# A planner in place of a hand-written order: causal attention and a feed-forward layer on one core

## The chip, the core and the metric

The kernel runs on one core of a Trainium2 chip. The core has five engines with a queue of their own each: TensorE (PE in the rows; PEld is its weight loads), VectorE (DVE), ScalarE (ACT), GpSimd (POOL) and SyncE (SP), which here issues every DMA. Each engine takes its instructions strictly in the order in which they stand in its queue. The metric is the device time of one execution, in microseconds.

## The reference

Four batches of 448 positions, 12 heads of 64. Causal attention in fp32, then layer normalising, then a feed-forward layer of width 3072 with a residual:

```python
scores = scale * np.matmul(q, k.transpose(0, 1, 3, 2))
scores = np.where(mask, -1000000000.0, scores)
scores = scores - np.max(scores, axis=-1, keepdims=True)
attn = np.exp(scores)
attn = attn / (np.sum(attn, axis=-1, keepdims=True) + 1e-09)
attn_out = np.matmul(attn, v)
x = attn_out.transpose(0, 2, 1, 3).reshape(B, S, H * D)
xn = (x - mu) / np.sqrt(var + 1e-06) * g_ln
return x + np.maximum(xn @ w_ch1, 0.0) @ w_ch2
```

The weights w_ch1 and w_ch2 arrive as 64-bit floats; the kernel makes fp32 of them on the chip.

## The kernel before

**Split products.** A large product is done in three passes: each operand is split into a high part (rounded to the fast matmul format, `wh`, `xh`, `hh`, `kh`) and a low part (the rest: `wl`, `xl`, `hl`, `kl`), and high x high, high x low and low x high are added in one PSUM bank. Making a pair of parts is a cast on ACT (L152, L659) and a subtraction on DVE (L156, L660) or POOL (L254, L425, L714).

**Attention** (class `Att`) goes by pairs of heads, six in a batch. For a pair: scores `sc` (L278 in full fp32 for batch 0, L285 split for the others), mask and row minimum on DVE (L293), exponential with its sum on ACT (L307), reciprocal on DVE and normalising (`norm`, L323, on POOL for batch 0, else on DVE), transposes `pt` of P on TensorE (L339), whose result is copied from PSUM to `PT` by ACT (L342) or DVE (L344), as a table `ev` says, and the product with V, `px` (L358): four blocks of columns (448, 336, 224, 112) for each of the two heads, which write to different halves of the bank. `stats` transposes x (`pln`, L371) for mean and variance.

**The stages.** Batch 0's attention stands alone at the start. Then `ffn` runs batches 0 and 1 (`ph` L490 to the hidden layer, `po` L509 out of it: 2 x 864 matmuls of 448 columns). In its `yield`s, once for 18 matmuls, pieces of the attention of batches 1, 2 and 3 are issued. In between, each weight tile is converted (L125, L129, L136), split, and stored: `scratch` holds the fp32 weight, `kept` both split parts, for later use. Last comes class `Pair`: batches 2 and 3 together by a scheme with 7 products in place of 8 on blocks. A group of it has two blocks of the first kind (7 products of 9 matmuls) and three of the second (7 of 6), 2 x 63 + 3 x 42 = 252 matmuls, and there are six groups. Sums of weight blocks (`s`, on POOL, L642) are split afresh (`wp`), single blocks are read from `kept` (`wk`). The products land in banks `bX`, `bY`, `bA`; `after1` combines them (copies `p1`, `u2`, `p5`, `b11`, `b22`, `b21` to SBUF on ACT, L706; sums on DVE, L709, L714, L717) and splits the hidden layer into `h1`, `h2`, `hx` parts; `after2` adds to `xT` (L779).

**What sets the order.** All by hand: tables at the top give each step of a head pair its slot (`SAT`, `TAT`, `NAT`, `END`, `STARTS`), a slot is one step of the loop over weights, and what is called first in a slot stands first in every queue it uses. `weights_ahead` places conversion and split some slots early; `Pair` loads and splits a set number of products ahead and lets a few steps lag by one or two products (`then`).

Of the kernel before, what the change touches and what calls it, by code (L numbers as in the profile page):

```python
# [1 line left out]

# [32 lines left out]
GAP = 6  # L35
FIRST = -20
# [21 lines left out]

@with_exitstack
def kernel(ctx, tc, qk, v, w1, w2, g, out):  # L60
    nc = tc.nc

    def pool(name, bufs, **kw):
        return ctx.enter_context(tc.tile_pool(name=name, bufs=bufs, **kw))
# [4 lines left out]
    ps_open, conv_open, att_open = ExitStack(), ExitStack(), ExitStack()  # L69
    ps = ps_open.enter_context(tc.tile_pool(name="ps", bufs=2, space=PSUM))  # L70
    conv = conv_open.enter_context(tc.tile_pool(name="conv", bufs=1))
    ap = att_open.enter_context(tc.tile_pool(name="ap", bufs=1, side="right"))
    late = []
# [16 lines left out]
    kept = [dr.tile([P, 2, UH], F32, name=f"kept{i}") for i in range(ns)]  # L90
# [54 lines left out]
    def keep_parts(s):  # L145
        for part, w in ((0, wh), (1, wl)):
            nc.sync.dma_start(out=kept[s % ns][:, part, :], in_=w[s].bitcast(F32))

    def split1(s):
        assert s in ready or s >= ns  # L150
        wh[s] = sb.tile([P, UH], F32R, tag="wh", name="wh", bufs=4)
        nc.scalar.activation(out=wh[s], in_=w32[s], func=ACTF.Copy)  # L152
# [7 lines left out]
    def open_late(_):  # L160
        conv_open.close()
        late.append(pool("late", 1, reuse_waits="tile"))

    def weights_ahead(start):
# [9 lines left out]
        for s in range(2 * ns):  # L174
            if s >= ns + KEEP0:
                put(s - 3, (load_parts, s))
                continue
            t = (-EARLY + GAP * s, *ELAG) if s < early else (s - 4, 1, 2, 3)
            put(t[0] + t[3], (split2, s))
            if s >= KEEP0:  # L180
# [24 lines left out]
    class Att:  # L205
# [31 lines left out]
        def split1(self, p):  # L237
# [5 lines left out]
            nc.scalar.activation(out=qs, in_=rq, func=ACTF.Copy)  # L243
            nc.vector.tensor_copy(kh, rk)  # L244
# [68 lines left out]
        def norm(self, p, h):  # L313
# [7 lines left out]
            for i in (0, 1, 3, 2):  # L321
                pp = self.t["P", p, h][:, OFF[i]:OFF[i + 1]]
                eng.tensor_scalar(  # L323
                    out=pp, in0=pp, scalar1=r[:, i:i + 1], scalar2=1.0,
                    op0=ALU.mult, op1=ALU.mult,
                )

        def transposes(self, p, grp, eng):
# [12 lines left out]
            if eng == "act":  # L341
                nc.scalar.copy(out=t[:, :o], in_=pt[:, :o])  # L342
            else:
                nc.vector.tensor_copy(t[:, :o], pt[:, :o])  # L344

        def pv(self, p):
# [15 lines left out]
            nc.scalar.copy(out=self.xT[p], in_=px)  # L362
# [49 lines left out]
        def apply1(self, c):  # L412
# [9 lines left out]
            nc.scalar.activation(out=self.xh[:, c, :], in_=t, func=ACTF.Copy)  # L422
# [55 lines left out]
    def ffn(a, s, hh, hl):  # L478
        for f0, f1 in ((0, HF), (HF, NF)):
            for x in range(0, HF, 2):  # L480
# [4 lines left out]
                for k, (y, c) in enumerate(seq):  # L485
                    if k == KC:
                        yield
# [6 lines left out]
                    if c == KC - 1:  # L494
# [4 lines left out]
                        )  # L499
                s += 2  # L500
                yield
            for m in range(KC):
                pm = ps.tile([P, S], F32, tag="mm", name="po", bufs=3)
                for x in range(HF):
                    if x == KC:
                        yield
# [12 lines left out]
    class Pair:  # L519
# [18 lines left out]
        def open_inputs(self):  # L538
            att_open.close()
            self.xp = pool("pair_x", 1, side="right", reuse_waits="tile")  # L540
# [13 lines left out]
        def parts(self, src, hi, lo, eng):  # L554
            nc.scalar.activation(out=hi, in_=src, func=ACTF.Copy)
# [29 lines left out]
        def plan(self):  # L585
# [21 lines left out]
            self.u, self.w, self.bank, self.hid = {}, {}, {}, {}  # L607
# [24 lines left out]
        def combine(self, b):  # L632
            w = self.width(b)
            u = self.u.pop(b)
            u = {(i, k): u[:, i, k * w:(k + 1) * w] for i in range(2) for k in range(2)}
# [9 lines left out]
        def weight_parts(self, n):  # L645
# [5 lines left out]
            t = sb.tile([P, 2, w], F32, tag=("wh", "wl")[n % 2], name="wk", bufs=4)  # L651
            nc.sync.dma_start(out=t, in_=kept[s][:, :, o:o + w])
            self.w[b, k] = t.bitcast(F32R)

        def weight(self, n):
# [3 lines left out]
            nc.scalar.activation(out=t[:, 0, :], in_=src, func=ACTF.Copy)  # L659
# [40 lines left out]
        def after1(self, b, blk, k):  # L700
# [4 lines left out]
            def copy(dst, src, func=ACTF.Copy):  # L705
                nc.scalar.activation(out=dst, in_=src, func=func)  # L706
# [21 lines left out]
            def then(lag, f, *args):  # L728
                self.later.setdefault(self.n + lag, []).append((f, args))
# [71 lines left out]
    with tc.manual_schedule():  # L801
# [4 lines left out]

        def add_batch(b):
# [12 lines left out]
            for mine, whole in ((first, pre), (second, post)):  # L820
                for t, fs in mine.items():
                    whole.setdefault(slot(t), []).extend(fs)
# [9 lines left out]
        make_identity(nc, ident)  # L832
# [9 lines left out]
        for s in range(start, 2 * ns):  # L842
            for b in range(1, B):
# [10 lines left out]
            for f, x in later:  # L854
                f(x)
            if s >= 0:
# [5 lines left out]
                next(feed)  # L862
            for f, args in post.get(s, []):
                f(*args)
# [14 lines left out]
        ps_open.close()  # L879
        psb = pool("psb", 8, space=PSUM, reuse_waits="tile")  # L880
        pair.hidden()
        pair.run()

# [32 lines left out]
```

## Time and profile before

| | us |
|---|---|
| median of 3 runs | 920.6 (918.53 to 920.83) |
| profiled execution | 918.47 |
| its span, first to last instruction | 916.6 |
| TensorE busy in it | 869.5 (95%) |
| DVE busy | 649.8 (71%) |
| ACT busy | 476.7 (52%) |
| POOL busy | 275.7 (30%) |

Busy is the time in which at least one instruction of the engine is at work. Matmuls overlap, each row being longer than the distance to the next, so that a TensorE at 100% is not yet at its best pace. What remains of the 916.6 us is time in which TensorE waits.

### The profile page before, as it was taken

What the parts mean: (1) busy time and instruction counts of PE and PEld (TensorE: products, weight loads), DVE (VectorE), ACT (ScalarE), POOL (GpSimd) and SP (SyncE); (2) the same over time, 40 slices, a digit from 0 to 9 for tenths busy, and PEclk for the clock granted to TensorE, in tenths of its full rate; (3) what the DMA queues carried; (4) which work ended last, traced back from release to release, by engine and by line L of the source; (5) the groups of instructions that cost most, each with busy time, mean ns of one, the idle gap of its engine ahead of it and who ended that gap; (6) DMA issues with size and microseconds to landing.
All of it is one profiled execution on the core that took longest, in us unless ns stands there. A gap on an engine that the chain in (4) does not pass through costs nothing.

```text
span 916.6 us, 13600 instructions
## 1 busy us (share of the span) xinstructions
PE 869.5 (95%) x4662; PEld 749.8 (82%) x4662; DVE 649.8 (71%) x1412; ACT 476.7 (52%) x1050; POOL 275.7 (30%) x274
## 2 busy tenths in 40 slices
PE   6989999999889989989999999899999999999998
PEld 4657988888768768878888889788889898888987
DVE  4876888767778987767667537877575856757585
ACT  6945888779667555544545312352433525243350
POOL 5643111111021221111111004755353525535440
PEclk9999999999899999999999999999999999999999
DMA  9911777768678978776887558635445363644534
GB/s 246 358 57 49 251 284 274 277 245 320 247 247 284 351 256 337 273 256 235 292 290 281 182 182 273 208 113 180 127 139 162 119 193 104 191 128 138 155 91 174
DMA packets 77876, 196.31 MB, mean 214 GB/s; under 512 B 7536, under 2 KB 35184, under 8 KB 77808
## 3 DMA queue, kind: packets, MB, share of 16 engines
q1 hardware_dynamic: 77808, 195.46, 62.1%
q8 instruction: 36, 0.59, 0.3%
q14 instruction: 32, 0.26, 0.1%
HBM read 133.30 MB, written 62.13 MB: 213 GB/s over the span
## 4 chain that ended last, share of the span: by engine, by line
PE 63%; ACT 14%; DVE 14%; DMA 4%; issue 4%; SPq 1%; POOL 0%; ACTq 0%; DVEq 0%
PE ph L490 15%; PE bX L695 14%; PE po L509 13%; PE bY L695 6%; PE px L358 4%; PE bA L695 3%; PE sc L285 3%; PE pt L339 3%; ACT P L307 2%; DVE wp L660 2%; ACT h L706 2%; DMA scratch<-w 2%; DVE w L136 1%; ACT w L125 1%; ACT b L706 1%
## 5 line engine op out<-in xcount | busy, mean ns | idle before, releaser
L254 POOL TENSOR_TENSOR kl<-qkraw,kh 128x896 fp32r<-128x896 f32 x18 | 49.3, 2740 | 294.6 <-DVE kh L244 224.6
L307 ACT ACTIVATE P<-P,nm 112x448 f32<-112x448 f32 (+3 forms) x176 | 91.7, 524 | 47.3 <-DVE nm L293 47.3
L490 PE MATMUL ph<-xh,wh 128*128 128x448 f32 x288 | 107.6, 374 | 0.0
L490 PE MATMUL ph<-xl,wh 128*128 128x448 f32 x288 | 106.4, 369 | 0.7 <-POOL xl L425 0.7
L509 PE MATMUL po<-hh,wh 128*128 128x448 f32 x288 | 106.9, 371 | 0.0
L509 PE MATMUL po<-hh,wl 128*128 128x448 f32 x288 | 105.8, 367 | 0.2 <-DVE wl L156 0.2
L490 PE MATMUL ph<-xh,wl 128*128 128x448 f32 x288 | 105.9, 368 | 0.0
L509 PE MATMUL po<-hl,wh 128*128 128x448 f32 x288 | 105.5, 366 | 0.0
L660 DVE TENSOR_TENSOR wp<-s,wp 128x256 fp32r<-128x256 f32 (+1 forms) x120 | 76.8, 645 | 33.8 <-ACT wp L659 32.2
L659 ACT ACTIVATE wp<-s 128x256 fp32r<-128x256 f32 (+1 forms) x120 | 53.7, 459 | 86.4 <-PE bY L695 41.9
L293 DVE CUSTOM_DVE_ANT_0 P<-sc,mask 112x448 f32<-112x448 f32 (+3 forms) x176 | 70.6, 444 | 29.9 <-PE sc L285 16.6
L714 POOL TENSOR_TENSOR h<-b,h 128x448 fp32r<-128x448 f32 x36 | 41.3, 1148 | 126.8 <-ACT b L706 82.2
L496 DVE SCALAR_TENSOR_TENSOR hl<-ph,hh 128x448 fp32r<-128x448 f32 x48 | 29.8, 623 | 65.8 <-ACT hh L495 65.5
L779 DVE TENSOR_TENSOR xT<-xT,bX 128x448 f32<-128x448 f32 x72 | 44.6, 619 | 34.5 <-PE bX L695 33.9
L339 PE MATMUL pt<-ident,P 112*112 112x112 f32 x440 | 55.0, 261 | 14.1 <-DVE stat L374 8.1
L339 PEld LDWEIGHTS pt<-ident,P 112*112 112x112 f32 x440 | 46.1, 133 | 24.7 <-DVE stat L374 9.3
L642 POOL TENSOR_TENSOR s<-u 128x256 f32<-128x256 f32 (+1 forms) x60 | 57.0, 951 | 25.0 <-DMA u<-scratch 14.7
L490 PEld LDWEIGHTS ph<-xl,wh 128*128 128x128 f32 x288 | 54.7, 190 | 5.6 <-POOL xl L425 1.3
L509 PEld LDWEIGHTS po<-hh,wl 128*128 128x128 f32 x288 | 54.1, 188 | 5.8 <-DVE wl L156 1.1
L490 PEld LDWEIGHTS ph<-xh,wh 128*128 128x128 f32 x288 | 54.7, 190 | 4.9
L509 PEld LDWEIGHTS po<-hh,wh 128*128 128x128 f32 x288 | 54.1, 188 | 5.3
L490 PEld LDWEIGHTS ph<-xh,wl 128*128 128x128 f32 x288 | 54.5, 189 | 4.6 <-DVE wl L156 0.3
(160 smaller groups left out, 2113.5 us busy)
## 6 DMA issues: line engine op xcount, KB each, us to landing
raw<-w_dram SPq DMA_DIRECT2D x39, 768.0 KB, 8.8
scratch<-w SPq DMA_DIRECT2D x48, 384.0 KB, 6.2
kept<-wh SPq DMA_DIRECT2D x48, 384.0 KB, 8.5
kept<-wl SPq DMA_DIRECT2D x48, 384.0 KB, 8.3
qkraw<-qk_dram SPq DMA_DIRECT2D x18, 896.0 KB, 6.1
full<-scratch SPq DMA_DIRECT2D x18, 768.0 KB, 8.7
wk<-kept SPq DMA_DIRECT2D x36, 384.0 KB, 3.8
wk<-kept SPq DMA_DIRECT2D x54, 256.0 KB, 3.2
```

The lines of the kernel that those rows point to most:

```text
L254: nc.gpsimd.tensor_tensor(out=kl, in0=rk, in1=kh.bitcast(F32), op=ALU.subtract)
L293: nc.vector.tensor_tensor_reduce(out=self.t["P", p, h][:, OFF[i]:OFF[i + 1]], in0=pt[:, o:o + n], in1=mask[:, S - n:], op0=ALU.add, op1=AL ...
L307: nc.scalar.activation(out=pp, in_=pp, func=ACTF.Exp, scale=-1.0, bias=nm[:, x:x + 1], accum_out=self.t["sm", p, h][:, i:i + 1],)
L339: nc.tensor.transpose(pt[:, o:o + C], pp[:, a:a + C], ident[:C, :C])
L490: nc.tensor.matmul(pm[y], lhsT=w[:, c * P:c * P + P], rhs=z[:, c, :], start=(c == 0 and i == 0), stop=(c == KC - 1 and i == 2),)
L509: nc.tensor.matmul(pm, lhsT=w[:, o:o + P], rhs=z[:, x, :], start=(x == 0 and i == 0), stop=(x == HF - 1 and i == 2),)
L642: nc.gpsimd.tensor_tensor(out=v[dst], in0=x, in1=y, op=op)
L659: nc.scalar.activation(out=t[:, 0, :], in_=src, func=ACTF.Copy)
L660: nc.vector.tensor_tensor(out=t[:, 1, :], in0=src, in1=t[:, 0, :].bitcast(F32), op=ALU.subtract)
L695: nc.tensor.matmul(pm, lhsT=w, rhs=z, start=(new and c == 0 and i == 0), stop=(c == nk - 1 and i == 2), skip_group_check=True,)
L714: eng.tensor_tensor(out=dst, in0=src, in1=y, op=ALU.subtract)
L779: nc.vector.tensor_tensor(out=t, in0=t, in1=src, op=ALU.add)
```

## The change

The kernel's code now runs twice over, in a sense. First every call of an engine is only written down: `Plan.record` keeps it as a `Task` with the tasks that it depends on (`access` compares the pieces of buffers that are read and written, a PSUM bank as a whole), a price (`cost`) and, for matmuls, a due time: the sum of the matmul prices written down before it. Then `schedule` walks backwards, giving each task the time by which it is needed, and forwards as a list schedule: the engine that is free first takes, of the tasks that are ready, the one needed soonest. Last, `issue` makes the real calls in the order of planned start. In the profile all instructions thus have one line, L398.

Copies between any of SBUF and PSUM (`move`), and the normalising of batches 1 to 3, are written down with two ways (`either`): ACT or DVE, whichever engine takes it; the second way counts as needed 8000 ns later. Each buffer of a pool becomes a place of its own. `ffn` yields after 3 matmuls in place of 9 or 18, so that the attention's steps are written down in finer turn. The lags in `Pair` go. Of split weights only the low part is stored in `kept` and read again; the high part is cast again, from `scratch` (`full`) or from the loaded block `u`, which stays in its buffer for that.

```diff
+    def cost(self, t):
+        n, sbuf = t.size, [x for x in t.ins if x.buf.pool.space is None and x.idx.size > 8]
...
+        if t.engine == "tensor":
+            if t.method == "transpose":
+                return 0.84 * n, 200, False
+            if t.kw["rhs"].dtype == F32R:
+                return max(0.4531 * n + 2.5, 60), 200, False
+            return (0.42 if t.outs[0].p[1] - t.outs[0].p[0] == D else 1.69) * n, 200, False
+        if t.engine == "scalar":
+            return n / 1.4 + 220 + 190 * ("accum_out" in t.kw), 60, False
...
+    def schedule(self):
...
+        for t in (tasks[n] for n in reversed(line)):
+            x = t.due if t.engine == "tensor" else 1e9
+            for m in t.then:
+                x = min(x, need[m])
+            if t.engine == "sync":
+                x -= DMA_SLACK + t.lag / 300
+            elif t.engine and t.engine != "tensor":
+                x -= t.cost + t.lag + SLACK
+            elif t.engine and x < t.due:
+                x -= t.cost + t.lag + SLACK
+            need[t.n] = x
...
+            while soon[e] and soon[e][0][0] <= at:
+                _, n, more = heapq.heappop(soon[e])
+                if n not in start:
+                    heapq.heappush(avail[e], (need[n] + more, n))
+            n = heapq.heappop(avail[e])[1]
...
+            if t.port:
+                at = max(at, port)
+                port = at + t.cost
...
+    def move(dst, src):
+        nc.either(
+            ("scalar", "activation", (), dict(out=dst, in_=src, func=ACTF.Copy)),
+            ("vector", "tensor_copy", (dst, src), {}),
+        )
...
     def load_parts(s):
-        for part, w, tag in ((0, wh, "wh"), (1, wl, "wl")):
-            t = sb.tile([P, UH], F32, tag=tag, name=tag, bufs=4)
-            nc.sync.dma_start(out=t, in_=kept[s % ns][:, part, :])
-            w[s] = t.bitcast(F32R)
+        t = sb.tile([P, UH], F32, tag="wl", name="wl", bufs=4)
+        nc.sync.dma_start(out=t, in_=kept[s % ns])
+        wl[s] = t.bitcast(F32R)
...
-            t = sb.tile([P, 2, w], F32, tag=("wh", "wl")[n % 2], name="wk", bufs=4)
-            nc.sync.dma_start(out=t, in_=kept[s][:, :, o:o + w])
-            self.w[b, k] = t.bitcast(F32R)
+            self.w[b, k] = t = sb.tile([P, 2, w], F32R, tag=("wh", "wl")[n % 2], name="wk", bufs=4)
+            move(t[:, 0, :], self.full[b][LEFT[k]])
+            nc.sync.dma_start(out=t[:, 1, :].bitcast(F32), in_=kept[s][:, o:o + w])
```

**First place: TensorE while batch 0's second half of the hidden layer is made.** `pt` and `pln` go to PSUM banks that ACT or DVE must empty, `sc` are scores of a later pair, `ph` matmuls of the hidden layer. Before:

```order
L339 MATMUL pt<-ident,P 112x112 x8
L371 MATMUL pln<-ident,xT 112x128 x2
L285 MATMUL sc<-kh,qs 112x224
L285 MATMUL sc<-kl,qs 112x224
L285 MATMUL sc<-kh,qs 112x224
L285 MATMUL sc<-kl,qs 112x224
L285 MATMUL sc<-kh,qs 112x448
L285 MATMUL sc<-kl,qs 112x448
L490 MATMUL ph<-xh,wh 128x448
L490 MATMUL ph<-xl,wh 128x448
```

The same transposes and statistics after the change:

```order
L398 MATMUL pt<-ident,P 112x112 x4
L398 MATMUL ph<-xh,wh 128x448
L398 MATMUL ph<-xl,wh 128x448
L398 MATMUL ph<-xh,wl 128x448
L398 MATMUL pt<-ident,P 112x112 x4
L398 MATMUL ph<-xh,wh 128x448
L398 MATMUL ph<-xl,wh 128x448
L398 MATMUL ph<-xh,wl 128x448
L398 MATMUL pln<-ident,xT 112x128 x2
L398 MATMUL ph<-xh,wh 128x448
L398 MATMUL ph<-xl,wh 128x448
L398 MATMUL ph<-xh,wl 128x448
```

The eight transposes, two statistics and six scores stood in one block; now three `ph` stand between each two pieces.

**Second place: ACT at the same transposes.** The two copies `PT<-pt` belong to the eight transposes above. Before:

```order
L125 ACTIVATE w32_2666<-raw_2487 128x768
L129 ACTIVATE bits_2665<-raw_2487 128x768
L152 ACTIVATE wh_2672<-w32_2556 128x768
L495 ACTIVATE hh_1013<-ph_2612 128x448
L342 COPY PT_2695<-pt_2694 112x448
L342 COPY PT_2702<-pt_2701 112x448
```

And after:

```order
L398 ACTIVATE hh_994<-ph_2520 128x448
L398 ACTIVATE P_2409<-P_2409,r_2536 112x224
L398 ACTIVATE P_2581,sm_2600<-P_2581,nm_2582 112x448
L398 ACTIVATE P_2581,sm_2600<-P_2581,nm_2592 112x336
L398 ACTIVATE PT_2617<-pt_2602 112x448
L398 ACTIVATE PT_2623<-pt_2612 112x448
L398 ACTIVATE wh_2631<-w32_2512 128x768
```

The copies stood behind the weight conversion, a cast and the `hh` of the block; now that cast stands behind them.

**Third place: the second block of a group in the pair.** ACT before, where `p1` is the copy of bank bX that lets TensorE go on in that bank:

```order
L706 ACTIVATE h1_6234<-bX_7681 128x448
L706 ACTIVATE h2_6235<-bY_7738 128x448
L706 ACTIVATE p1_7828<-bX_7816 128x448
L706 ACTIVATE h1_6234<-bZ_7771 128x448
L706 ACTIVATE h2_6235<-bA_7833 128x448
```

DVE after, where that copy now stands:

```order
L398 TENSOR_TENSOR bZ_7795<-b21_7830,bZ_7795 128x448
L398 COPY p1_7852<-bX_7828 128x448
L398 TENSOR_TENSOR h2_6351<-bY_7757,h2_6351 128x448
L398 TENSOR_TENSOR wp_7855<-s_7751,wp_7855 128x256
L398 TENSOR_TENSOR h1_6241<-bZ_7795,h1_6241 128x448
L398 TENSOR_TENSOR bA_7850<-bA_7850,p1_7852 128x448
```

The copy has changed engine. Some products later in the same block, DVE before, up to the step `bA<-bY`, from which the hidden layer's parts are made:

```order
L717 TENSOR_TENSOR bY_7870<-bY_7870,u2_7868 128x448
L660 TENSOR_TENSOR wp_7895<-s_7748,wp_7895 128x256
L717 TENSOR_TENSOR bZ_7898<-bX_7816,p5_7883 128x448
L660 TENSOR_TENSOR wp_7916<-s_7748,wp_7916 128x256
L709 SCALAR_TENSOR_TENSOR bA_7833<-bY_7870,b11_7846 128x448
```

And DVE after:

```order
L398 CAST wp_7914<-s_7751 128x256
L398 TENSOR_TENSOR bY_7887<-bY_7887,u2_7890 128x448
L398 TENSOR_TENSOR bZ_7925<-bX_7828,p5_7904 128x448
L398 TENSOR_TENSOR wp_7914<-s_7751,wp_7914 128x256
L398 SCALAR_TENSOR_TENSOR bA_7850<-bY_7887,b11_7885 128x448
```

The subtraction of a weight stands ahead of `bA<-bY` in both; its cast, which ACT did, is now DVE's own.

## Rows read from the trace of the kernel before

**Rows 1.** The windows; columns as the first line says (PEclk: granted clock).

```profile
core 0: us, PE busy (x) PEld busy (x) DVE busy (x) ACT busy (x) POOL busy (x), PEclk, DMA share, GB/s
0.00:79.97 79.97, 66.50 (x383) 44.21 (x383) 52.80 (x181) 52.26 (x148) 38.33 (x72) 0.98 0.61 190
79.97:200.00 120.03, 119.90 (x673) 105.30 (x674) 92.77 (x202) 97.58 (x185) 17.13 (x10) 1.00 0.66 243
200.00:360.00 160.00, 143.96 (x823) 123.84 (x822) 129.54 (x291) 106.25 (x220) 28.60 (x14) 0.98 0.80 292
360.00:585.60 225.60, 221.89 (x1272) 195.04 (x1272) 148.81 (x359) 96.95 (x222) 41.05 (x26) 1.00 0.72 253
585.60:916.60 331.00, 317.25 (x1515) 281.36 (x1513) 225.92 (x382) 123.69 (x277) 150.62 (x154) 1.00 0.47 145
sum 916.60, PE 869.50 PEld 749.76 DVE 649.82 ACT 476.73 POOL 275.74; mean PE 173.90 PEld 149.95 DVE 129.96 ACT 95.35 POOL 55.15
```

**Rows 2.** The chain that ended last: start us, length us, what, count.

```profile
353.23 2.04 PE px L358 x16
381.95 3.67 PE ph L490 x18
...
754.63 1.84 PE bX L695 x9
```

**Rows 3.** TensorE's waits, 200 to 360: us in total, times, longest.

```profile
PE pt L339 <- DVE stat L374: 5.5, 3, 2.4
PE pln L371 <- ACT PT L342: 4.1, 2, 3.7
```

**Rows 4.** TensorE in order of time: start, length, what, [idle before <-releaser].

```profile
235.89 0.93 PE L339 MATMUL pt<-ident,P 112*112 112x112 f32 x8
240.56 0.68 PE L371 MATMUL pln<-ident,xT 128*112 128x128 f32 x2 [3.75 <-ACT PT L342]
...
243.28 0.57 PE L490 MATMUL ph<-xh,wl 128*128 128x448 f32 x1
```

**Rows 5.** ACT in order of time, at the same place.

```profile
237.27 0.89 ACT L125 ACTIVATE w<-raw 128x768 f32<-128x768 f32 x1
...
239.99 0.94 ACT L342 COPY PT<-pt 112x448 f32<-112x448 f32 x2
```

**Rows 6.** DVE in order of time, at the same place.

```profile
240.12 0.62 DVE L496 SCALAR_TENSOR_TENSOR hl<-ph,hh 128x448 fp32r<-128x448 f32 x1 [2.12 <-ACT hh L495]
```

**Rows 7.** The chain, one group of the pair before the row at 754.63.

```profile
700.63 1.84 PE bX L695 x9
```

**Rows 8.** TensorE's first matmuls in order of time, and its last in the chain.

```profile
5.46 8.10 PE L278 MATMUL sc<-first_qk 128*112 128x448 f32 x22 [5.46 <-DMA first_qk<-qk_dram]
...
911.75 1.25 PE bX L695 x6
```

**Rows 9.** TensorE in order of time, in the second block of a group.

```profile
767.89 0.47 PE L695 MATMUL bX<-xT2h,wp 128*128 128x448 f32 x1 [0.41 <-ACT p L706]
```

**Rows 10.** ACT in order of time, at the same place.

```profile
767.26 0.58 ACT L706 ACTIVATE p<-bX 128x448 f32<-128x448 f32 x1
```

**Rows 11.** DVE in order of time, in the block before.

```profile
762.27 1.20 DVE L660 TENSOR_TENSOR wp<-s,wp 128x384 fp32r<-128x384 f32 x1 [1.46 <-ACT wp L659]
763.39 0.62 DVE L709 SCALAR_TENSOR_TENSOR bA<-bY,b 128x448 f32<-128x448 f32 x1
```

**Rows 12.** DVE in order of time, in batch 0's attention.

```profile
45.81 4.05 DVE L251 TENSOR_TENSOR qs<-qkraw,qs 64x896 fp32r<-64x896 f32 x1
```

**Rows 13.** POOL in order of time, at the same place.

```profile
46.84 2.07 POOL L254 TENSOR_TENSOR kl<-qkraw,kh 128x896 fp32r<-128x896 f32 x1
```

**Rows 14.** Groups by line: count | busy us, mean ns | idle before, releasers.

```profile
L660 DVE TENSOR_TENSOR wp<-s,wp 128x256 fp32r<-128x256 f32 (+1 forms) x120 | 76.8, 645 | 33.8 <-ACT wp L659 32.2 <-POOL s L642 1.5
L642 POOL TENSOR_TENSOR s<-u 128x256 f32<-128x256 f32 (+1 forms) x60 | 57.0, 951 | 25.0 <-DMA u<-scratch 14.7 <-DVE xT L779 5.3 <-DVE wp L660 4.6
L659 ACT ACTIVATE wp<-s 128x256 fp32r<-128x256 f32 (+1 forms) x120 | 53.7, 459 | 86.4 <-PE bY L695 41.9 <-PE bX L695 40.4 <-POOL s L642 4.1
```

More of the change, by code (lines that the diff above doesn't have):

```diff
@@ L68, with turn, f @@
     dr = pool("dr", 1, space=DRAM)
[L69 to L73, printed above, removed]
+    ps = pool("ps", 2, space=PSUM)
+    conv = pool("conv", 1)
+    ap = pool("ap", 1, side="right")
+    late = [pool("late", 1, reuse_waits="tile")]
+    pair_x = pool("pair_x", 1, side="right", reuse_waits="tile")
+    psb = pool("psb", 8, space=PSUM, reuse_waits="tile")
+    def turn(old, new):
+        def f():
+            stacks[old.name].close()
+            open_pool(new)
+        plan.change(f, [old], [new])
     ident = const.tile([P, P], F32, name="ident")
@@ L89 @@
     scratch = [dr.tile([P, UE], F32, name=f"scratch{i}") for i in range(len(order))]
-    kept = [dr.tile([P, 2, UH], F32, name=f"kept{i}") for i in range(ns)]
+    kept = [dr.tile([P, UH], F32, name=f"kept{i}") for i in range(ns)]
     ready = set()
@@ L145, in keep_parts @@
     def keep_parts(s):
-        for part, w in ((0, wh), (1, wl)):
-            nc.sync.dma_start(out=kept[s % ns][:, part, :], in_=w[s].bitcast(F32))
+        if s < ns:
+            nc.sync.dma_start(out=kept[s], in_=wl[s].bitcast(F32))
+            return
+        kind, i = order[s // 2 - ns // 2]
+        ranges = [(0, UH)]
+        if kind == "w1" and i % 2:
+            ranges = [(UH // 2, UH)]
+        elif kind == "w2" and i // 2 % 2:
+            ranges = [(0, 2 * P), (4 * P, UH)] if s % 2 else [(2 * P, 4 * P)]
+        for a, b in ranges:
+            nc.sync.dma_start(out=kept[s - ns][:, a:b], in_=wl[s][:, a:b].bitcast(F32))
+    def move(dst, src):
[3 more added lines that the diff above has]
+        )
     def split1(s):
@@ L340, in transposes @@
                     o += C
[L341 to L344, printed above, removed]
+            move(t[:, :o], pt[:, :o])
         def pv(self, p):
@@ L361, in pv @@
                     )
-            nc.scalar.copy(out=self.xT[p], in_=px)
+            move(self.xT[p], px)
             self.done.add(("pv", p))
@@ L421, in apply1 @@
             )
-            nc.scalar.activation(out=self.xh[:, c, :], in_=t, func=ACTF.Copy)
+            move(self.xh[:, c, :], t)
         def apply2(self, c):
@@ L538, in open_inputs @@
         def open_inputs(self):
-            att_open.close()
-            self.xp = pool("pair_x", 1, side="right", reuse_waits="tile")
+            turn(ap, pair_x)
+            self.xp = pair_x
             self.at[0].parts()
@@ L805, with behind, g @@
         pre, post, att = {}, {}, {}
+        def behind(b, t, f):
+            def g(*args):
+                nc.wait = BEHIND if b and t < 0 else 0.0
+                f(*args)
+                nc.wait = 0.0
+            return g
         def add_batch(b):
@@ L821, in add_batch @@
                 for t, fs in mine.items():
-                    whole.setdefault(slot(t), []).extend(fs)
+                    whole.setdefault(slot(t), []).extend((behind(b, slot(t), f), a) for f, a in fs)
             return slot(min(min(first), min(second)))
@@ L861 @@
                     feed = ffn(att[s // ns], s, hh, hl)
-                next(feed)
-            for f, args in post.get(s, []):
-                f(*args)
+                for i in range(STEPS):
+                    next(feed)
+                    for f, args in todo[len(todo) * i // STEPS:len(todo) * (i + 1) // STEPS]:
+                        f(*args)
+            else:
+                for f, args in todo:
+                    f(*args)
             if s >= PAIR:
@@ L878 @@
             pass
-        ps_open.close()
-        psb = pool("psb", 8, space=PSUM, reuse_waits="tile")
+        turn(ps, psb)
         pair.hidden()
         pair.run()
+        for x in (const, sb, dr, ps, conv, ap):
+            open_pool(x)
+        plan.issue(tc.nc, plan.schedule()[0])
 def kernel(q, k, v, moe_g_ln, moe_w_ch1, moe_w_ch2):
```

341 lines of the change are left out of this document (315 added, 26 removed).

## The prediction

> **What bounds the kernel now.** I read the windows first, cut at the places where the program changes character: batch 0's attention (0 to 79.97 us, "A"), the two dense batches with the other batches' attention between their matmuls (79.97 to 585.6, "B", in three pieces), and the products of the pair (585.6 to the end, "C"). The reader should see in [rows 1] that TensorE is busy for 869.5 of 916.6 us and that no other engine comes near it in any piece; DMA is busiest at 0.80. So the kernel is bound by TensorE plus the time it stands still, and the question is how much of the standing still can go. The piece 79.97 to 200 has 0.13 us of it, 200 to 360 has 16.0: same matmuls, same neighbours, another moment. That is a sign of order, not of capacity.
>
> A busy TensorE overstates its work, since a matmul's row is longer than its slot. The slot is in the chain: 18 ph in 3.67 us, 9 bX in 1.84 us, so 0.204 us each, and 16 px pieces (one head pair) in 2.04 us [rows 2].
>
> What it waits for in the bad piece is in the list of waits: transposes and statistics waiting for a PSUM bank that DVE or ACT has not emptied [rows 3]. One case in order of time: 8 transposes at 235.89, then nothing until 240.56, 3.75 us put down to a PT copy [rows 4]. ACT has that copy in its queue behind a weight conversion that starts at 237.27 and two more casts, and reaches it at 239.99 [rows 5], while DVE, which could have copied, is idle for 2.12 us of that time [rows 6]. TensorE has 18 ph ready behind the waiting instruction, in the same queue.
>
> **The change, part by part.** (1) *Stage B, order of TensorE and of the copies.* The first two order pieces show the same place in both: eight transposes, two statistics and six scores in a row become groups of four, four and two with three ph between, and on ACT the two PT copies stand ahead of the cast that was before them. A copy late by 0.6 us is then covered by three ph (3 x 0.204). Idle time to win: 120.03 - 119.90, 160.00 - 143.96 and 225.60 - 221.89, so 0.1 + 16.0 + 3.7 = 19.9 us [rows 1]. The granted clock of 0.98 from 200 to 360 means that 0.04 x 160 = 6.4 us ran at 1.2 GHz instead of 2.4, which costs 3.2 us; the ph at 243.28, right behind the 3.75 us hole, takes 0.57 us [rows 4], and I let it go with the hole. Upper bound 23.1 us, lower bound 0 (or below, see the rivals). I take 19, because a piece with the same kinds of work already runs with 0.13 us of idle time [rows 1], less two px groups cut in B (part 5).
>
> (2) *Stage C.* Here TensorE's order hardly moves: three matmuls in each period of 252. One period runs from 700.63 [rows 7] to 754.63 [rows 2], 54.0 us, for work of 252 x 0.2044 = 51.5: 2.5 us lost per period, six times. In all C has 1512 matmuls, 309.1 us, between 585.6 and the last matmul's end at 913.0 (327.4 us) [rows 8]: 18.3 us to win at most. The losses have two addresses. bX waits 0.41 us for a p copy of its own bank [rows 9], which ACT starts only at 767.26 [rows 10], behind two h copies. And a weight subtraction on DVE waits 1.46 us for its cast on ACT, then takes 1.20 us, and the step bA <- bY, on which the next block's inputs hang, stands behind it at 763.39 [rows 11]. In the third place of the order both are met: p1 is copied by DVE, one step from the front; and the weight whose subtraction stands ahead of bA <- bY is now cast by DVE itself, three instructions earlier, so that it need not wait for ACT. The cost on the other side: 28 p and u copies move to DVE, at 0.62 us as for bA <- bY [rows 11], 17.4 us; 24 casts of weights on DVE, at no more than the 0.645 of its subtraction [rows 14], 15.5 us. DVE in C goes from 225.9 to 259 of some 318 us; ACT gains 84 casts at 0.459 [rows 14], 38.6 us, and loses 28 x 0.58 [rows 10] and 18 x 0.459, so 123.7 becomes 138. Neither becomes the bound. I take 12 of the 18.3, two of the 2.5 us in each of six periods; bounds 0 and 18.3.
>
> (3) *Stage A.* Idle besides the first load (5.46 us [rows 8]): 79.97 - 66.50 - 5.46 = 8.0 us, and the clock 0.98 costs 0.02 x 80 = 1.6 us, together 9.6 [rows 1]. One piece of it is the 4.05 us that DVE's qs subtraction took while POOL ran kl [rows 12, 13]. But the end of A is a serial chain (last pair, statistics, their root, normalising, split) that no order shortens, and 11 of the 13 new cuts in px are here. Six of them put the first 448 columns of one head alone: 2.04 x 448/1120 = 0.82 us each, 4.9 us, of which some falls into gaps. I take a gain of 9.6 - 4.9 = 5; bounds 0 and 9.6.
>
> (4) *DMA.* Only the low parts of the split weights are kept and read again (51 writes in place of 96, and half of each read); the high part is cast again from a tile that stands in SBUF anyway. The DMA share is 0.47 in C and at most 0.80 in B [rows 1], and TensorE waits for a DMA at the first load [rows 8], so I price this at 0 in time; the cover is the share that is left, and without it the loads would be shorter, not longer. The casts it adds are in part 2.
>
> (5) *Cut px groups in B*: two cuts, 0.82 each at most: +1, inside the 19 of part 1.
>
> (6) *The rest* (constants made in place, pools with one buffer for each place, the lags of the pair's steps dropped): the same work in another order, 0; what covers small additions is the fifth of C that DVE has free.
>
> Sum on the profiled execution: 918.47 - 5 - 19 - 12 = 882.5 us. That execution lies 2.1 us under the median of the runs (920.6), and their lowest is 918.53. I add most of that and say 884 us.
>
> **A rule against the change.** DVE's qs took 4.05 us [rows 12]: it starts at 45.81 and ends just under 1 us after POOL's kl ends at 46.84 + 2.07 = 48.91 [rows 13]. The Trainium skill, "SBUF — State Buffer", section "SBUF: two separate sides", says why: DVE, when it reads two SBUF operands or runs in a two-port mode, and POOL take one shared port pair as an exclusive lock for a whole instruction. The trace agrees, with those 4.05 us. The change gives DVE more such work (casts from SBUF to SBUF). By the rule alone C could grow; it is the third rival.
>
> **The rivals.** *First: only B is cleared.* C keeps its 2.5 us per period, since TensorE's order there stands and the gaps come at the same places in every period; A keeps its chain. Then 918.47 - 19 = 899.5, about 901 as a median. For it: the waits in C are on a bank's release, and eight banks are all there are. Against it: the copy that is late there is late in ACT's own queue [rows 10], and that queue is changed. On such a repeating gap the Trainium skill, "Perfetto Trace Analysis", section "Optimization Strategy", says that it can mean too few buffers; by it this rival's 901 would be the result, and the trace speaks for it only as far as the releaser is a bank's copy [rows 9]. Chance 0.18.
>
> *Second: it moves waits and removes none on balance.* The order is fixed from prices. They hold for matmuls (0.4531 x 448 + 2.5 = 205.5 ns, against 204), but a px group is priced at 0.42 ns x 2240 columns = 0.94 us and takes 2.04 [rows 2]. Every instruction behind a px in the plan comes 1.1 us later than planned, 24 times, 26 us; if queues of DVE and ACT are tied to it by their fixed order, new gaps replace the old: 917 to 921 us. Against it: a late TensorE makes weights and copies early, not late. Chance 0.05.
>
> *Third: slower, by the shared port in C.* POOL is busy for 150.6 us of C [rows 1] with operations of 0.951 us [rows 14]. If each of the 116 weight subtractions (of 120 in [rows 14]) and 24 casts that DVE does in C has to sit out one whole POOL operation, that adds 140 x 0.951 = 133 us to DVE's 259: 392, and DVE bounds C instead of TensorE, 61 us over the 331 of now: 918.5 - 24 + 61 = 955. It decides from 0.69 us per operation: then 259 + 96 = 355, which eats the 24 us won in A and B. The subtraction's mean now holds some waiting already, 0.645 in all [rows 14], so 0.69 more is far off. Chance 0.05.
>
> **How the numbers follow.** Forecast 0.72, its own range 868 (every recoverable microsecond: 918.47 - 9.6 - 23.1 - 18.3 = 867.5) to 894; first rival 0.18 at 901; second 0.05; third 0.05. The range for 8 in 10 leaves out the last two and a little of the first's upper side: 867 to 905. No change is within 0.3%, 2.8 us. Faster: 0.72 + 0.18 = 0.90; same 0.04 (most of the second); slower 0.06.
>
> **What would show it.** Right: between 200 and 360 us TensorE's idle time falls from 16 us to a few, and pt and pln no longer head its list of waits; the clock shows 1.00 there; periods of C fall from 54.0 to about 52; the first ph comes at 73 to 76 us instead of 79.97; B's length falls from 505.6 to about 487. Wrong: periods of C still at 54 (first rival); subtractions of weights on DVE with a mean far over 0.645 us and DVE idle nowhere in C (third); waits of TensorE for weights, wl or wh, in B, which the old order hardly has; or a first ph as late as before. What would overturn the forecast altogether is a TensorE idle time near the old 47 us, only elsewhere.

## The result, and the profile after

The changed kernel takes 881.59 us (median of 4 runs, 880.19 to 881.73) where the kernel before takes 919.57 (917.45 to 920.83): ratio 0.9586, 95% interval 0.9563 to 0.9609. The forecast was 884 us, and 882.5 for the profiled execution, which took 880.19 (span 878.40).

The windows of the kernel after, cut as in [rows 1], but with one difference: 80.20 us is the first `ph`, while the 79.97 of [rows 1] is the second, behind its wait for `xl`. The first `ph` of the kernel before starts at 78.84.

```profile
core 0: us, PE busy (x) PEld busy (x) DVE busy (x) ACT busy (x) POOL busy (x), PEclk, DMA share, GB/s
0.00:80.20 80.20, 68.87 (x382) 43.97 (x383) 45.96 (x177) 52.84 (x151) 36.50 (x72) 0.98 0.60 179
80.20:200.00 119.80, 119.06 (x655) 104.26 (x656) 100.18 (x197) 100.27 (x186) 14.94 (x9) 0.97 0.71 264
200.00:360.00 160.00, 157.91 (x923) 136.44 (x922) 132.96 (x298) 130.70 (x276) 28.44 (x15) 1.00 0.71 255
360.00:567.68 207.68, 207.68 (x1194) 181.74 (x1193) 153.44 (x331) 96.50 (x218) 42.54 (x31) 1.00 0.54 186
567.68:878.40 310.72, 307.03 (x1513) 283.35 (x1511) 239.41 (x429) 139.34 (x308) 143.56 (x148) 1.00 0.37 111
```

TensorE is busy throughout from 360 us to its last matmul. To split the gain I measure between starts of TensorE's instructions: A to the first `ph`, B from there to the last `po`, C from the first product of the pair to its last.

| | first matmul | A | B | C |
|---|---|---|---|---|
| before | 5.46 | 78.84 | 506.93 | 326.65 |
| after | 6.51 | 80.20 | 487.28 | 306.67 |
| change | +1.05 | +1.36 | -19.65 | -19.98 |
| forecast | | -5 | -19 | -12 |

The waits of TensorE after, in B (us in total, times, longest):

```profile
PE pln L398 <- ACT PT L398: 1.8, 1, 1.8
PE ph L398 <- POOL xl L398: 0.7, 1, 0.7
PE pt L398 <- ACT PT L398: 0.3, 1, 0.3
```

In C the list is empty, where it read before:

```profile
PE bX L695 <- ACT p L706: 5.7, 7, 2.9
PE bX L695 <- DVE xT L779: 2.3, 6, 0.4
PE bY L695 <- DVE xT L779: 1.5, 6, 0.3
```

[rows 9] is one of the seven waits for `p`. The twelve for DVE's sums into `xT`, 3.8 us, stand in no step of the prediction.

The 1.8 us in B is the only hole left of the sort in [rows 4]. In order of time, four transposes behind a `po`, and then a statistic that waits for the `PT` copy with nothing placed between:

```profile
317.85 0.37 PE L398 MATMUL po<-hl,wh 128*128 128x448 f32 x1
318.49 0.59 PE L398 MATMUL pt<-ident,P 112*112 112x112 f32 x4 [0.27 <-ACT PT L398]
320.90 0.32 PE L398 MATMUL pln<-ident,xT 128*112 128x128 f32 x1 [1.82 <-ACT PT L398]
```

The chain after, where [rows 2, 7] were read (start, length, what):

```profile
681.09 3.66 PE bX L398 x18
...
732.30 3.66 PE bX L398 x18
```

The same place of two successive groups: the period is 51.2 us, not 54.0.

A got longer although order and choice rule there too. TensorE in order of time, batch 0; the cut `px` groups, and then the end of A:

```profile
28.78 0.96 PE L398 MATMUL px<-PT,rest 112*64 112x448 f32 x2
30.96 2.10 PE L398 MATMUL px<-PT,rest 112*64 112x448 f32 x14
...
74.60 1.19 PE L398 MATMUL mb<-ident,mv 112*128 112x112 f32 x6
77.18 1.63 PE L398 MATMUL rb<-ident,ve 112*128 112x112 f32 x8 [1.39 <-POOL ve L398]
80.20 1.11 PE L398 MATMUL ph<-xh,wh 128*128 128x448 f32 x2 [1.38 <-ACT xh L398]
82.05 0.74 PE L398 MATMUL ph<-xl,wh 128*128 128x448 f32 x1 [0.74 <-POOL xl L398]
```

A group cut in two takes 0.96 + 2.10 where a whole one takes 2.11 in the same view (before, from 30.27). And the idle matmuls, which stood between `mb`, `rb` and `ph` before (at 75.03 and 77.15), now stand ahead of them, from 68 to 74 us. Windows of TensorE at that place (us, busy, granted clock, DMA share, GB/s):

```profile
75.00:80.00 5.00, 2.41 (x13) 0.77 0.30 120
80.00:90.00 10.00, 9.06 (x28) 0.60 0.16 44
```

The granted clock falls from 2.4 to 1.2 GHz at 77.67 us, just behind the first of the three holes (1.39 us), and rises at 87.91, after almost 6 us of `ph` without a hole. In between the `ph` take 0.37 us each, not 0.20.

### The profile page after: what moved, and what is told of

Read it like the earlier page. It is cut to its first block, busy times and chain, and to the rows that moved or that the text cites. A ratio compares the mean times of both kernels' runs of the same rounds, so it can differ in the third digit from the quotient of the medians.

```text
span 878.4 us, 13759 instructions
## 1 busy us (share of the span) xinstructions
PE 860.5 (98%) x4662; PEld 749.8 (85%) x4662; DVE 672.0 (76%) x1429; ACT 519.7 (59%) x1135; POOL 266.0 (30%) x274
## 4 chain that ended last, share of the span: by engine, by line
PE 97%; DVE 1%; DMA 0%; ACT 0%; POOL 0%; SPq 0%; issue 0%; POOLq 0%; DVEq 0%; ACTq 0%
PE ph L398 21%; PE po L398 20%; PE bX L398 20%; PE bY L398 10%; PE sc L398 7%; PE px L398 6%; PE pt L398 5%; PE bA L398 5%; PE pln L398 1%; DMA first_qk<-qk_dram 0%; PE rb L398 0%; PE idle L398 0%; PE mb L398 0%; POOL xl L398 0%; POOL ve L398 0%; DVE xT L398 0%
## 5 line engine op out<-in xcount | busy, mean ns | idle before, releaser
L398 POOL TENSOR_TENSOR kl<-qkraw,kh 128x896 fp32r<-128x896 f32 x18 | 40.9, 2270 | 283.9 <-ACT kh L398 246.1
L398 DVE CUSTOM_DVE_ANT_0 P<-sc,mask 112x448 f32<-112x448 f32 (+3 forms) x176 | 73.8, 444 | 54.2 <-PE sc L398 52.9
L398 PE MATMUL ph<-xh,wh 128*128 128x448 f32 x288 | 113.0, 397 | 1.4 <-ACT xh L398 1.4
L398 PE MATMUL po<-hh,wh 128*128 128x448 f32 x288 | 108.4, 383 | 0.0
L398 PE MATMUL ph<-xl,wh 128*128 128x448 f32 x288 | 106.5, 370 | 0.7 <-POOL xl L398 0.7
L398 PE MATMUL ph<-xh,wl 128*128 128x448 f32 x288 | 106.3, 370 | 0.0
L398 ACT ACTIVATE P<-P,nm 112x448 f32<-112x448 f32 (+3 forms) x176 | 90.9, 519 | 23.8 <-DVE nm L398 23.7
L398 PE MATMUL po<-hh,wl 128*128 128x448 f32 x288 | 104.2, 367 | 0.0
L398 PE MATMUL po<-hl,wh 128*128 128x448 f32 x288 | 104.0, 366 | 0.0
L398 ACT ACTIVATE wp<-s 128x256 fp32r<-128x256 f32 (+1 forms) x102 | 46.8, 467 | 69.6 <-PE bX L398 31.5
L398 POOL TENSOR_TENSOR s<-u 128x256 f32<-128x256 f32 (+1 forms) x60 | 55.3, 922 | 92.3 <-DMA u<-scratch 82.2
L398 ACT ACTIVATE wk<-u 128x256 fp32r<-128x256 f32 (+1 forms) x84 | 38.6, 462 | 70.6 <-PE bX L398 50.9
L398 ACT ACTIVATE PT<-pt 112x448 f32<-112x448 f32 x90 | 48.2, 541 | 41.8 <-PE pt L398 38.8
L398 DVE TENSOR_TENSOR wp<-s,wp 128x256 fp32r<-128x256 f32 (+1 forms) x120 | 67.7, 573 | 2.4 <-ACT wp L398 1.5
L398 PEld LDWEIGHTS pt<-ident,P 112*112 112x112 f32 x440 | 49.9, 133 | 14.9 <-issue 2.3
L398 PE MATMUL pt<-ident,P 112*112 112x112 f32 x440 | 61.6, 260 | 0.3 <-ACT PT L398 0.3
L398 PEld LDWEIGHTS ph<-xh,wh 128*128 128x128 f32 x288 | 54.9, 191 | 6.8 <-ACT xh L398 1.6
L398 POOL TENSOR_TENSOR h<-b,h 128x448 fp32r<-128x448 f32 x36 | 43.1, 1197 | 54.7 <-ACT h L398 33.4
L398 PEld LDWEIGHTS ph<-xh,wl 128*128 128x128 f32 x288 | 54.9, 191 | 5.0
L398 PEld LDWEIGHTS ph<-xl,wh 128*128 128x128 f32 x288 | 55.2, 192 | 4.4 <-POOL xl L398 1.4
L398 PEld LDWEIGHTS po<-hh,wh 128*128 128x128 f32 x288 | 54.1, 188 | 4.8
L398 PEld LDWEIGHTS po<-hh,wl 128*128 128x128 f32 x288 | 54.0, 188 | 4.5
```

Of the source, the lines that this page charges most:

```text
L398: getattr(getattr(nc, t.engine), t.method)(*args, **kw)
```

## Experiments

In the table, ratios are against the kernel before on the same chip, with 95% intervals; A, B and C are from the profiled execution. The kernel before took 920.7 to 922.2 us as a median in these sessions, so that times 2 us apart are read by their ratios.

| | us | ratio | A | B | C |
|---|---|---|---|---|---|
| after | 881.59 | 0.9586 [0.9563, 0.9609] | 80.20 | 487.28 | 306.67 |
| c_fixed | 880.63 | 0.9566 [0.9538, 0.9595] | 81.01 | 486.46 | 306.36 |
| all_fixed | 888.04 | 0.9640 [0.9612, 0.9669] | 81.60 | 493.95 | 306.21 |
| rec_fixed | 970.27 | 1.0540 [1.0504, 1.0575] | 78.98 | 522.12 | 363.55 |
| rec_free | 983.54 | 1.0685 [1.0644, 1.0727] | 82.32 | 538.21 | 355.58 |
| both_parts | 898.23 | 0.9748 [0.9726, 0.9770] | 81.09 | 504.61 | 306.55 |
| low_twice | 897.45 | 0.9750 [0.9713, 0.9786] | 80.22 | 502.72 | 306.59 |
| both_fast_bus | 882.86 | 0.9592 [0.9562, 0.9623] | 82.72 | 486.26 | 307.26 |
| before_no_high | 921.30 | 1.0006 [0.9987, 1.0024] | 80.49 | 506.80 | 327.17 |
| idle_dep | 879.25 | 0.9542 [0.9522, 0.9561] | 80.12 | 485.16 | 306.93 |
| px_price | 877.61 | 0.9526 [0.9507, 0.9544] | 77.54 | 487.15 | 307.48 |
| px_whole | 875.31 | 0.9500 [0.9479, 0.9521] | 75.37 | 486.41 | 306.53 |
| idle_and_whole | 874.90 | 0.9512 [0.9478, 0.9546] | 75.44 | 486.09 | 306.99 |

**Order or choice of engine?** The first gives the pair's copies back to ACT, the second all copies to their old engines; in both the schedule makes a new order for the engines so fixed. Here and below, `...` stands for lines left out:

```diff
-    def move(dst, src):
+    def move(dst, src, free=True):        # c_fixed: the pair passes False
+        if not free:
+            nc.scalar.activation(out=dst, in_=src, func=ACTF.Copy)
+            return
...
```

> The changed kernel, but every copy of the pair (parts of the inputs, weights' high parts, p1, u2, p5, T1 to T4) is ACT's again, as before the change; the order is still a list schedule. As predicted (the gain in C has two addresses, p1 on DVE and the weight casts on DVE): both addresses come back, the pair takes 318 to 326 us instead of 306.7, period 53 to 54, total 893 to 901 us, and TensorE's list of waits in C has bX on ACT's p and DVE's subtractions wait for ACT's wp again. Rival (the order alone clears C, whichever engine copies): C stays at 307 to 309, total 881 to 884.

```diff
-    def move(dst, src):
-        nc.either(
...
+    def move(dst, src, eng="act"):        # all_fixed: kh and some PT pass "dve"
+        if eng == "act":
+            nc.scalar.activation(out=dst, in_=src, func=ACTF.Copy)
+        else:
+            nc.vector.tensor_copy(dst, src)
...
```

> The changed kernel with no choice of engine at all: each copy and each normalising is on the engine that it had before the change, the new wk casts on ACT; the list schedule orders all. As predicted: B keeps most of its 19.6 us (length 487.5 to 492, since TensorE's order with ph between the transposes does it), C returns to 318 to 326, total 895 to 906 us. Rival one (order alone): 881 to 886 in all. Rival two (the choice does it, the order moves waits only): B back at 500 to 507, C at 326, total 912 to 921.

My theory of C falls: with ACT doing every copy, C is 306.36 us, and TensorE waits for nothing there. What was late is on time by its place in the queue. In c_fixed DVE, in order of time, around the step `bA<-bY` of [rows 11]:

```profile
730.84 0.56 DVE L398 TENSOR_TENSOR wp<-s,wp 128x384 fp32r<-128x384 f32 x1
732.02 0.63 DVE L398 SCALAR_TENSOR_TENSOR bA<-bY,b 128x448 f32<-128x448 f32 x1 [0.62 <-PE bY L398]
```

ACT in the same kernel, the copy of [rows 10], and TensorE's product that needs it [rows 9]:

```profile
730.28 0.53 ACT L398 ACTIVATE wp<-s 128x384 fp32r<-128x384 f32 x1 [0.94 <-PE bX L398]
...
735.44 0.57 ACT L398 ACTIVATE h<-bY 128x448 fp32r<-128x448 f32 x1
735.86 0.58 ACT L398 ACTIVATE p<-bX 128x448 f32<-128x448 f32 x1
```

```profile
737.31 0.36 PE L398 MATMUL bX<-xT2h,wp 128*128 128x448 f32 x1
```

At this place ACT casts the weight early enough that DVE's subtraction waits for nothing, `bA<-bY` now waits for TensorE alone, and the whole row of steps behind it moves forward. The copy `p` is still behind the `h` copies, but those are done sooner: it starts 1.45 us before the product that needs its bank, where before it started 0.63 us before it and made it wait. Counted from the start of the last product in bY (761.62 before, 731.62 in c_fixed), `bA<-bY` starts 1.37 us sooner and `p` 1.40. So at this place `p` was late because the weight's cast and subtraction were, and no engine had to change. That is read from one place; a kernel that moves the cast alone was not run, and in all of C DVE still waits for ACT's `wp` at 12 places (16.8 us; 32.2 us at 23 before) without making TensorE wait. The choice is worth something only outside C: all_fixed loses 6.7 us in B, 3.8 of them in two waits of `po` for `wh` on ACT and some 3 by the clock, which is at half speed for 13.7 us of B there and for 7.7 in the changed kernel.

The next two take the schedule's order away; what was written down is issued in that order, with the dependences kept:

```diff
-        plan.issue(tc.nc, plan.schedule()[0])
+        plan.schedule()                   # engines chosen, order dropped
+        plan.issue(tc.nc, plan.recorded())
```

> The engines are those that the schedule chose, but the instructions are issued in the order in which they were written down, not in that of the schedule. If the order carries the gain: 912 to 930 us, with TensorE idle 40 us or more again, in B and in C. If the choice of engines carries it: 882 to 895.

> Neither schedule nor choice: written-down order, engines as before the change. What is left of the change is the finer turns (a step of the attention after every 3 matmuls instead of 9 or 18), the dropped lags, constants made in place, and low parts alone kept and read. If these are worth nothing, as predicted: 912 to 930 us. Rival (the finer turns carry the gain of B, since three ph stand between a transposing step and the next even so): B 487 to 492, total 890 to 900.

Both lose more than I had allowed, in B and C alike: the written order is now only raw material for the schedule (the pair's lags are gone), no plan of its own, so these runs bound nothing against the kernel before. They show that the written order, with its finer turns, does not carry the gain, and that engines chosen for one order are worse than the old ones in another (983.5 against 970.3). What finer turns would do to the kernel before was not run.

**The DMA term.** Both parts kept and read again, as before the change, under the new schedule:

```diff
-            nc.sync.dma_start(out=kept[s], in_=wl[s].bitcast(F32))
+            for part, w in ((0, wh), (1, wl)):
+                nc.sync.dma_start(out=kept[s][:, part, :], in_=w[s].bitcast(F32))
...
```

> High and low parts of the split weights are kept and read again, as before the change; no cast of wk (84) nor of the last 12 weights of B. The schedule and the choice stay. As predicted (DMA priced at 0): 879 to 883 us, C 306 to 308. Rival one (the halved traffic is what cleared C, whose DMA share fell from 0.47 to 0.37): C back to 312 to 325, 886 to 899. Rival two (the casts cost): 2 to 4 us less.

Neither I nor the rivals had this: C is untouched, and B gives back 17.3 of its 19.65 us (some 4.5 of them by the clock, at half speed for 16.7 us of B). TensorE's windows in both_parts (columns as above):

```profile
250.00:300.00 50.00, 50.00 (x305) 1.00 0.90 329
300.00:360.00 60.00, 51.03 (x268) 0.91 0.65 234
```

DMA at 0.90 with 329 GB/s, and 9 us of holes right behind it, look like a chip that can't move the bytes. But the changed kernel moves nearly as much in the same 50 us and has 2.1 us of holes behind it:

```profile
250.00:300.00 50.00, 50.00 (x301) 1.00 0.88 320
300.00:360.00 60.00, 57.91 (x335) 1.00 0.63 219
```

The loads of `raw` weights between 200 and 360 us land 9.3 us after their issue in both_parts (median), 9.1 in the changed kernel. And the schedule itself reckons with 320 bytes per ns of DMA and orders everything by that. So three more kernels: the same with 400 in its place; the changed kernel with each low part written twice; and the kernel before without the writes of high parts.

```diff
-                bus = max(bus, at + 1300) + t.lag / 320
+                bus = max(bus, at + 1300) + t.lag / 400
...
```

> As both_parts (898.2 us, B 504.6 instead of 487.3), but the schedule reckons with 400 bytes per ns of DMA instead of 320. If the 17 us were lost because the transfers themselves do not get through (DMA share 0.90 and 329 GB/s between 250 and 300 us in both_parts): the kernel stays at 893 to 902 us, and TensorE waits for weights (wh) in B, now unplanned. If they were lost in the plan, which reckoned a queue of transfers that the chip does not have, and put weights late for it: B back at 485 to 490, 879 to 884 us.

```diff
-            nc.sync.dma_start(out=kept[s], in_=wl[s].bitcast(F32))
+            for dst in (kept, again):
+                nc.sync.dma_start(out=dst[s], in_=wl[s].bitcast(F32))
...
```

> The changed kernel, but each low part is written a second time to a place that is never read: as many bytes written as in both_parts, the high part's buffers not held by any transfer, reads as in the changed kernel. If bytes (on the chip or in the plan's reckoning) cost the 17 us of both_parts: B 500 to 506, 893 to 899 us. If it was the buffers of the high parts, held until their transfer has landed: B 487 to 490, 881 to 885 us.

```diff
-        for part, w in ((0, wh), (1, wl)):
-            nc.sync.dma_start(out=kept[s % ns][:, part, :], in_=w[s].bitcast(F32))
+        nc.sync.dma_start(out=kept[s % ns][:, 1, :], in_=wl[s].bitcast(F32))
...
```

> The kernel before, without the 48 writes of high parts; where the high part was read, the unsplit weight is read from scratch instead (so the values of these weights are not rounded; in the pair two transfers of half the size in place of one). If the halved writes gave the change its gain in B whatever the order: B 488 to 495 instead of 506.9, 903 to 912 us. If before's waits were waits for copies in a fixed order, as predicted: B 503 to 508, 915 to 923 us, and between 200 and 360 TensorE still stands still for 13 to 17 us, most of it for pt and pln.

The windows of both_fast_bus, with the same transfers as both_parts:

```profile
250.00:300.00 50.00, 50.00 (x305) 1.00 0.89 301
300.00:360.00 60.00, 59.37 (x340) 1.00 0.83 293
```

The chip moves the bytes (0.83 in the second window), and B is 486.26. The 17 us were in the order that the schedule made out of its own price for DMA; low_twice, in which no transfer holds a buffer of a high part, loses most of them too (15.4), so those buffers are not the cause. Within what I can tell, the added transfers themselves cost nothing (0.9592 against 0.9586); the changed kernel with the price of 400 was not run. The old order gains nothing from fewer writes: in before_no_high TensorE still stands still for 13.5 us between 200 and 360, and its waits are those of [rows 3] (here from 200 to 480 us):

```profile
PE pt L340 <- DVE stat L375: 6.2, 4, 2.4
PE pln L372 <- ACT PT L343: 4.7, 4, 3.8
```

**The lost gain in A.** Idle matmuls tied to the statistics; the price of `px`; and `px` groups in one piece:

```diff
+        last = nc.tasks[-1].n             # idle_dep, in keep_busy
         for i in range(n):
             nc.tensor.matmul(...)
+            nc.tasks[-1].deps.add(last)
```

> The changed kernel, with each group of idle matmuls made to depend on the last statistics matmul ahead of it (6 on mb, 8 on rb), so that they lie in the holes of 75.8 to 77.2 and 78.8 to 80.2 us and not before them, as they did before the change. If the low clock of 77.67 to 87.91 us comes from these holes: the clock stays full there, 5.1 us less, 875 to 877 us in all, length of B 482 to 483 us, first ph still at 80 us. Rival (the clock falls for what lies earlier, and the idle matmuls between the statistics served something else): 880 to 882, the clock at half behind the first ph as now.

```diff
-            return (0.42 if t.outs[0].p[1] - t.outs[0].p[0] == D else 1.69) * n, 200, False
+            return (0.91 if t.outs[0].p[1] - t.outs[0].p[0] == D else 1.69) * n, 200, False
```

> Only the price of a px matmul is changed, from 0.42 to 0.91 ns per column, which is what a px group measured (2.04 us for 2240 columns). If wrong prices cost something (second rival of the prediction): the rows behind each px in the plan keep their order to what the chip does, holes at 50 to 58 us close, first ph at 76 to 79 instead of 80.2, total 876 to 880. If a price that is off on the bound engine costs nothing: 880 to 882.

```diff
+            n0 = len(nc.tasks)            # px_whole, in pv, around the eight matmuls
...
+            for t in nc.tasks[n0 + 1:] if self.b == 0 else []:
+                nc.tasks[n0].deps.update(n for n in t.deps if n < n0)
```

> In batch 0 the first matmul of a px group waits for all the copies that the group reads, so that the two heads' matmuls alternate. As predicted (11 cuts cost up to 0.82 us each, 4.9 us in sum for the six of 448 columns): TensorE's work to the first ph falls by 3 to 5 us, first ph at 76 to 77.5 instead of 80.2, total 876 to 878. Rival (the end of A is a serial chain, and the cuts fill time that was idle): first ph at 79.5 to 81.5, total 880 to 882.

px_whole is the largest step: A 80.20 to 75.37. TensorE in order of time there:

```profile
30.38 2.11 PE L398 MATMUL px<-PT,rest 112*64 112x448 f32 x16
...
71.64 2.05 PE L398 MATMUL rb<-ident,ve 112*128 112x112 f32 x8 [1.95 <-POOL ve L398]
75.37 1.12 PE L398 MATMUL ph<-xh,wh 128*128 128x448 f32 x2 [1.68 <-ACT xh L398]
```

The cuts thus cost 4.8 us of A: TensorE's busy time to the first `ph` falls by 5.6 us (68.87 to 63.26), of which 0.9 come back as idle time. px_price gains 2.7 us of A and keeps cuts; idle_dep shortens the half-speed stretch from 10.24 to 3.41 us and B by 2.1, less than half of what I expected, and its time alone is at the edge of what ratios tell. Then both together:

> idle_dep and px_whole together: idle matmuls that depend on the statistics, and px groups of batch 0 in one piece. If the two gains (2.3 and 6.3 us against the changed kernel's 881.6) come from different places, the clock behind the first ph and TensorE's work in A: 872 to 874 us, first ph at 75 to 76, B 484 to 485. If the clock falls for what lies earlier: 875 to 876.

They don't add. The windows of TensorE in px_whole, and then in idle_and_whole:

```profile
70.00:90.00 20.00, 16.57 (x64) 0.74 0.43 147
90.00:311.00 221.00, 221.00 (x1282) 1.00 0.73 271
311.00:320.00 9.00, 6.91 (x41) 1.00 0.84 293
```

```profile
70.00:90.00 20.00, 16.98 (x84) 1.00 0.42 145
90.00:311.00 221.00, 220.74 (x1282) 1.00 0.74 274
311.00:320.00 9.00, 7.18 (x33) 0.81 0.82 264
```

The clock holds behind the first `ph`, as expected, but falls behind the 1.8 us hole 240 us later, which px_whole has too without a fall. That takes back 1.7 us (3.41 us at half speed). And there was less to win than I reckoned: in both kernels the first `ph` with `xl` starts only at 76.6 us, so that half speed could cost px_whole 2.6 us, from there to 81.89. Of the 1 us that remains, B shows 0.3 and C is 0.5 longer, which is within the spread of C over these kernels (306.2 to 307.5). px_whole and idle_and_whole beat both kernels: 875 us, 0.950 to 0.951.

## Why the prediction was right or wrong

*The sum* was right to 2.3 us, but by luck, by two errors of opposite sign: A came out 6.4 us worse than its term, C 8.0 better. Only B was right as a term.

*B* (-19, measured -19.65): cause and place as predicted; the old waits for `pt` and `pln` are gone but at one place, and before_no_high keeps them. Two things were not in the step. The schedule wins 6.7 us of B only with the engines' choice (all_fixed), and 17.3 us only while its price for DMA does not bind (both_parts). And the half-speed stretch behind the first `ph` lies in B: 7.7 us of it (80.20 to 87.91), so some 3.9 us of gain were lost there. The step had counted the old stretch's 3.2 us as won; that 19 was met even so, with 4 of its 23.1 us held back for other reasons, is in part luck too.

*C* (-12, measured -19.98): the failed step is "the losses have two addresses" with its remedy, `p1` and the casts on DVE. Both addresses were real places of lateness [rows 9 to 11]; the remedy was not what cleared them: with all copies on ACT, C is 306.36 us (c_fixed). A third, TensorE's waits for `xT`, the step did not have. Having moved work in view, I took the visible change of engine for the cause and the mere change of position beside it for none. The bound "18.3 us to win at most" was also too small. It used 0.2044 us per matmul from rows of 9 and 18; C now runs at 306.67 / 1511 = 0.2030, which over 1512 matmuls is 2.1 us (0.4 go the other way: the first product starts at 585.97, not 585.6). Holding some of C back as unwinnable had no row behind it: TensorE has no wait left there. The price of the moved work was on the safe side: DVE is busy for 239.4 us of C, not 259.

*A* (-5, measured +1.36): the term subtracted 4.9 us for cut `px` groups, which is what they cost (4.8), from a gain of 9.6, which was not there. Of the idle time behind the first load, 7.3 us before the first `ph`, the change won 2.5; TensorE's busy time grew by 2.8. (The 8.0 us of the term holds the wait for `xl` too, since it took 79.97 for the first `ph`.) Without cuts A gains 78.84 - 75.37 = 3.5 us. The first matmul comes 1 us later (6.3 to 6.6 in every kernel issued in the schedule's order, 5.5 in rec_free and rec_fixed, so the schedule's order is the cause), and the serial end of A stays: in px_whole `rb` still waits 1.95 us for `ve`, and `ph` 1.68 for `xh`. I had named that chain and still counted its idle time as winnable. The first `ph` "at 73 to 76" came true only in px_whole and idle_and_whole, which has the same edit.

*DMA* (0): right for the chip as far as both_fast_bus shows, wrong for the change. Halving the traffic was no saving in time but a condition under which this planner, with its price of 320, finds the good order.

*Rivals.* The first (only B is cleared, 901) is refuted by C's empty list of waits. The reading that it took from the Trainium skill, "Perfetto Trace Analysis", section "Optimization Strategy", that such a repeating gap can mean too few buffers, is not what the gap meant here: the eight banks are the same, and order closed the gap. The second (wrong prices move waits) exists, but small: px_price gains 2.7 us in A, and from 85 to 564 us TensorE then waits for nothing. The third (shared port) did not come. By lines (count | busy us, mean ns | idle before, releaser), where [rows 14] had 645 and 951 ns:

```profile
L398 DVE TENSOR_TENSOR wp<-s,wp 128x256 fp32r<-128x256 f32 (+1 forms) x120 | 67.7, 573 | 2.4 <-ACT wp L398 1.5
L398 POOL TENSOR_TENSOR s<-u 128x256 f32<-128x256 f32 (+1 forms) x60 | 55.3, 922 | 92.3 <-DMA u<-scratch 82.2 <-DVE wp L398 10.2
```

Each got shorter, and the idle time of DVE before `wp` fell from 33.8 to 2.4 us. In C after the change TensorE waits for nothing, so that the port set no time there. In the kernel before it seems to have had a part: the subtraction of [rows 11] took 1.20 us beside this step of POOL, and 0.56 in c_fixed (at 730.84), where POOL was idle:

```profile
761.91 1.15 POOL L714 TENSOR_TENSOR h<-b,h 128x448 fp32r<-128x448 f32 x1 [0.60 <-ACT b L706]
```

That agrees with the rule on the port in the Trainium skill, "SBUF — State Buffer", section "SBUF: two separate sides", as [rows 12, 13] do.

## What to carry to other kernels

Before an engine swap is credited with a gain, pin the engines and let the planner order them anew: here the order gave all of C and two thirds of B, and the choice 6.7 us. Where a planner sets the order, its prices are part of the kernel: a DMA price of 320 bytes per ns in place of 400 cost 18 us of B on the same traffic (504.61 against 486.26), and looked like a full DMA queue until the price alone was changed. List schedulers split groups that the hardware runs better whole, and pull filler work ahead of the hole that it was meant for; tie both down by dependences.

## What was not expected of the hardware

- `px` matmuls of 64 output columns, of two heads in turn, take 2.11 us for 16 (px_whole); with the first 2, of one head, issued apart it is 0.96 + 2.10 us for the same 16 (the changed kernel).
- Behind a hole of 1.82 us ahead of the same `pln`, after some 220 us in which TensorE had all but no hole, the granted clock fell to 1.2 GHz in idle_and_whole (at 314.33, for 3.41 us), and in px_whole and the changed kernel it stayed at 2.4.
- TensorE lost nothing over 50 us with 329 GB/s and a DMA share of 0.90 (both_parts), and 0.6 us over 60 with 293 GB/s and 0.83 (both_fast_bus).
